# Fused windowed attention and gated unit on one core: output tiles spread over the steps, separate banks and earlier transposes for the first pairs, one mask moved off VectorE

## The chip, the core and the metric

The kernel runs on one core of a Trainium2 chip. Its time is the device time of one execution in microseconds; the time before is 200.69 us, the median of three runs (199.18 to 202.72). The profile is of one more execution, which took 199.83 us and whose profiled span is 198.1 us. All positions "at x us" below are counted from the start of that span.

The engines are named as in the profile: PE is the matrix engine (PEld its weight loads), DVE the vector engine, ACT the scalar engine, POOL the general engine, SP the engine whose queue issues nearly all transfers (SPq).

## What is computed

Attention with a window over 8 batches, 8 heads, 576 positions and a head size of 64, then a gated unit with a causal convolution over the result. Heads 0 to 3 have a plain window of 32 keys; heads 4 to 7 have 32 keys at a distance of 4 (dilated). Cut to what matters:

```python
B, H, S, D = 8, 8, 576, 64
rel = pos[:, None] - pos[None, :]
mask_plain = (rel >= 0) & (rel < 32)
mask_dil = (rel >= 0) & (rel < 128) & (rel % 4 == 0)
attn = softmax(where(mask, q @ k.T / 8, -1e9)) @ v     # per head
x = attn.transpose(0, 2, 1, 3).reshape(B, S, 512)
gate = sigmoid(sum(conv_w[k] * x shifted by 4 - k for k in range(5)))
out = (gate * (x @ w_val)) @ w_out                      # float32
```

## The kernel before

**Pairs and steps.** The work is cut into 32 pairs of heads, four to a batch: c = 0 and 1 are plain, c = 2 and 3 dilated. The main loop has one step for each pair i. Two pairs of one batch and kind make a group g, so there are 16 groups; q, k and v are loaded by group. In a step from 8 on, PE computes the scores of pair i in two halves (L476), ACT takes the exponential (L518), DVE multiplies by the mask (L529), PE multiplies by v (`attn_v`, L531), and DVE normalises (L579, L580). Between these, each step has one convolution (`conv`, 24 matmuls, ACT takes the gate at L654), the transposes of an earlier pair's result (`trans_x`, copied by DVE at L614), transposes of the next group's k or q (`trans_main`, copied by ACT at L407, L404, L418), two value products (`val`, DVE multiplies by the gate at L676), and in some steps one output tile (`out_tile`, L682).

**Output tiles.** An output tile is 128 rows of the result: four matmuls with 512 columns (L687), one eviction on ACT (L692) into one of four buffers `osb`, and one or two stores from the SP queue (L698). There are 36, 18 for each half G of the rows. The values make them available over time, into the list `outs`. In the loop, the condition `c % 2 == 0 and i >= 10` runs one tile in each even step from 10 to 30. All others follow the last step: one after the convolution there, one after each of the last eight values, and the rest in a row.

**The order of the work.** There is no automatic scheduler: each engine executes its instructions in the order in which the program emits them, and each waits in that order. Steps 0 to 7 follow a small table, `program` (L745): X is the transposes of the pair before and its convolution's entry, T the transposes of the next pair's k and q, C a convolution, M and N the two masks, V a value, A the attention output with its normalisation, J a warming matmul, K, Q and R the transposes of group 4, U a cast of v on ACT, and D the convolution's diagonal weights.

**PSUM.** Scores use tiles of two banks, two in rotation (`ps_sc`); all else takes single banks, four in rotation (`ps_one`, through `bank()`). For pairs below `EARLY_AV` = 5 the attention output goes to two single banks, each normalised for itself (L586, L587); from pair 5 on it goes into the second scores tile of the pair, which is then free for the next scores only after L580.

**Transfers.** The SP queue issues loads and stores in program order. A group's loads (k, q, their remainders, v) are issued in even steps, three groups ahead. POOL casts v (`prep_v`, L199 to L208) and, for plain groups from 6 on, k and q (L186).

**The mask of the dilated heads.** `make_bias_d` (L314) is called in step 0. POOL builds bands of 0 and -32768. Its last 32 columns `mb` must also be closed where the parity of key and query differs: `same` holds 0 or -32768 (L263), and DVE takes the minimum (L326). For pairs below `EARLY_M` = 5 the bias is added in PE; later pairs are multiplied by a mask that POOL derives from it (L331).

Of the kernel before, what the change touches and what calls it, by code (L numbers as in the profile page):

```python
# [11 lines left out]
ALU = mybir.AluOpType  # L12
# [11 lines left out]
def kernel(  # L24
# [11 lines left out]
    nc = tc.nc  # L36
# [3 lines left out]
    K = moe_conv_w.shape[0]  # L40
    window = 32
    DIL = 4
    T = S // DIL
    TM = 128
    TR = T - TM
# [6 lines left out]
    CP = T + 2  # L52
    TB = 80
    NP = B * NCH
    EARLY_AV = 5
    EARLY_M = 5
    NEG = -32768.0

# [22 lines left out]
    same = consts.tile([128, 2], BF16, name="same")  # L81
    par_i = consts.tile([128, 2], I32, name="par_i")
# [31 lines left out]
    def bank():  # L114
        return ps_one.tile([128, 512], FP32, name="ps_bank")
# [58 lines left out]
    def load_group(g):  # L174
        for name in ("k", "q"):
            load_main(g, name, 0, 4, nc.sync)
        for name in ("k", "q"):
            load_rest(g, name, nc.sync)
        load_v(g)
# [39 lines left out]
    def pair_info(i):  # L219
        b, c = i // NCH, i % NCH  # L220
        dil = int(c >= NCH // 2)
        return b, c, dil, 2 * b + dil, (c % 2) * 2

    def load_pair(g, a):
        load_main(g, "k", a, a + 2, nc.sync)
        load_main(g, "q", a, a + 2, nc.sync)
        if a == 0:
            load_rest(g, "k", nc.sync)
            load_rest(g, "q", nc.sync)
        load_v(g, a, a + 2)  # L230
# [20 lines left out]
        out=ident, in_=ident, compare_op=ALU.not_equal, fill=1.0,  # L251
        base=0, pattern=[[-1, 128]], channel_multiplier=1,
# [4 lines left out]
        out=ident5, in_=ident5, compare_op=ALU.not_equal, fill=1.0,  # L257
        base=0, pattern=[[-1, 8]], channel_multiplier=1,
    )
    nc.gpsimd.iota(par_i, pattern=[[1, 2]], base=1, channel_multiplier=1)  # L260
    nc.vector.tensor_scalar(out=par_i, in0=par_i, scalar1=1, scalar2=None, op0=ALU.bitwise_and)

    nc.vector.tensor_scalar(  # L263
        out=same, in0=par_i, scalar1=-NEG, scalar2=NEG, op0=ALU.mult, op1=ALU.add)
    for ke in kEs:
        nc.vector.memset(ke[:, :, 0, 96:128], 0.0)
    for et in ets:
# [5 lines left out]
    def band(dst, pattern, base, cm=1):  # L273

        nc.gpsimd.memset(dst, 0.0)
        nc.gpsimd.affine_select(
            out=dst, in_=dst, compare_op=ALU.is_ge, fill=NEG,
            base=base, pattern=pattern, channel_multiplier=-cm,
        )
        nc.gpsimd.affine_select(  # L280
            out=dst, in_=dst, compare_op=ALU.is_ge, fill=NEG,
            base=window - 1 - base, pattern=[[-s, n] for (s, n) in pattern],
            channel_multiplier=cm,
        )
# [4 lines left out]
    for (z, dst) in ((0, bias_1), (1, btmp)):  # L289
# [5 lines left out]
        out=mh, in_=mh, compare_op=ALU.is_ge, fill=0.0,  # L295
        base=96, pattern=[[-1, 2], [1, 4], [4, 24]], channel_multiplier=-2)
# [8 lines left out]
    def make_perm():  # L305

        nc.gpsimd.memset(perm, 0.0)
        pv = perm.rearrange("p (w t) -> p w t", w=2)
        for (x, n, base) in ((0, 16, 0), (16, 32, -32)):
            nc.gpsimd.affine_select(  # L310
                out=pv[:, :, x:x + n], in_=pv[:, :, x:x + n], compare_op=ALU.not_equal, fill=1.0,
                base=base, pattern=[[-n, 2], [-1, n]], channel_multiplier=1)

    def make_bias_d():  # L314
        band(bias_d[:, 0:TM], [[1, TM]], 0)
        nc.gpsimd.tensor_copy(bias_d[:, TM:2 * TM], bias_d[:, 0:TM])

        mb = bias_d[:, 2 * TM:HB].rearrange("p (w t) -> p w t", w=2)
        nc.gpsimd.memset(mb, 0.0)
        for (lo, up) in ((True, 0), (False, 0)):  # L320
            sg = 1 if lo else -1
            base = 2 * (TM - TB) if lo else 2 * (window - 1) - 2 * (TM - TB)
            nc.gpsimd.affine_select(
                out=mb, in_=mb, compare_op=ALU.is_ge, fill=NEG, base=base,
                pattern=[[sg, 2], [2 * sg, TR]], channel_multiplier=-sg)
        nc.vector.tensor_tensor(  # L326
            out=mb, in0=mb, in1=same[:, :, None].to_broadcast([128, 2, TR]), op=ALU.min)

    def make_masks():
        for (m, x) in ((mask_p, bias_p), (mask_d, bias_d)):  # L330
# [20 lines left out]
    def load_weight(src):  # L351
        nc.sync.dma_start(out=w_st, in_=src.rearrange("(c p) n -> p c n", p=128))
# [168 lines left out]
    def apply_mask(i, hf):  # L521
        if i < EARLY_M:
            return
        b, c, dil, g, a = pair_info(i)
        et = st[(i, "et")]
        e3 = et[:, hf, 0:2 * HB].rearrange("p (h n) -> p h n", h=2)
        m = mask_d if dil else mask_p[:, 3 * hf:3 * hf + 3, :].rearrange("p n q -> p (n q)")
        m = m[:, None, :].to_broadcast([128, 2, HB])
        nc.vector.tensor_tensor(out=e3, in0=e3, in1=m, op=ALU.mult)  # L529

    def attn_v(i, hf):  # L531
# [3 lines left out]
        et = st[(i, "et")]  # L535
        if i >= EARLY_AV:
            ps = [st[(i, 1)][:, f, :] for f in range(2)]
# [30 lines left out]
    def normalize(i):  # L568
# [6 lines left out]
        else:  # L575
            dst = xn[0:R].rearrange("p z n h d -> p z (n h) d")
        if i >= EARLY_AV:
            av = st[(i, 1)][0:R, :, 0:6 * AVS].rearrange("p f (x e) -> p f x e", x=6)
# [103 lines left out]
    def out_tile(G, n):  # L682
        w = w_out_b if G == 0 else w_out_s
        ps = bank()
        y0 = 128 * n % (YB * HB)
        for c in range(NCH):
            nc.tensor.matmul(  # L687
                out=ps, lhsT=y_half[G][:, c, y0:y0 + 128], rhs=w[:, c, :],
                start=(c == 0), stop=(c == NCH - 1),
            )  # L690
        osb = out_pool.tile([128, Dm], FP32, name="osb")
        nc.scalar.mul(out=osb, in_=ps, mul=0.5)  # L692
        p = 0
        while p < 128:
            f = 128 * n + p
            b, r, t = f // HB, 2 * G + (f % HB) // T, f % T
            w = min(128 - p, T - t)
            nc.sync.dma_start(  # L698
                out=out[b].rearrange("(t r) n -> r t n", r=4)[r, t:t + w, :],
                in_=osb[p:p + w, :])  # L700
            p += w


    convs, vals, outs = [], [], []
# [16 lines left out]
            outs.append((G, done_out[G]))  # L721
            done_out[G] += 1

    def run_out():
        out_tile(*outs.pop(0))

    def warm(n):
        for _ in range(n):
# [2 lines left out]
    EARLY = 8  # L731

    def next_pair(i, names=("k", "q", "rest")):
# [13 lines left out]
        "X J U J T A J",  # L747
        "X T A J J",
        "X A C C D D J T",
        "X C M N T V V A",  # L750
        "C V M N V X T V A V",
        "C M N X V V A T",
        "C M N X K A Q R J",
    ]
    diags = [2, 3]

# [44 lines left out]
    for i in range(NP):  # L801
        b, c, dil, g, a = pair_info(i)

        if i == 0:
            load_weight(moe_w_val)
            load_pair(2, 0)
        elif i == 1:
            load_pair(2, 2)
        elif i == 2:
            load_pair(3, 0)  # L810
        elif i == 3:
            load_pair(3, 2)
            load_group(4)
        elif i == 4:
            load_weight(moe_w_out)
        if c % 2 == 0 and 5 <= g + 3 < 2 * B:
            load_group(g + 3)

        if i == 0:
            prep_v(0)  # L820
            make_bias_d()
            prep_v(1)
            make_perm()
        elif i < 3:
            prep_v(i + 1)
            if i == 2:
                make_masks()
        elif i == 3:
            cast_val()
            prep_v(4)  # L830
        elif i == 4:
            prep_v(5)
            prep_v(6)
        elif i == 5:
            prep_v(7)
        elif i > 6:
            if i == 8:
                cast_out()
            elif 8 < i < 13:
                for h in range(2):  # L840
                    swap_out(h, i - 9)
            if i < NP - 1:
                prep_v(i + 1)
            if g + 2 < 2 * B and g % 2 == 0:
                cast(g + 2, "k" if a == 0 else "q")
            if 12 <= i < 16:
                swap_val(i - 12)
        scores(i, 0)
        if i == 0:
            trans_rest(0)  # L850
            setup_conv_w()
        scores(i, 1)
        if i == 0:
            make_conv_diag(0)
            make_conv_diag(1)
        if i < EARLY:
            early_rest(i)
            continue
        run_conv(i - 1)
        apply_mask(i, 0)  # L860
        after_x(i - 1)
        if g + 1 < 2 * B:
            trans_main(g + 1, "k" if a == 0 else "q")
        apply_mask(i, 1)
        if c > 0 and vals:
            run_val()
        attn_v(i, 0)
        attn_v(i, 1)
        normalize(i)
        if a == 0 and g + 1 < 2 * B:  # L870
            trans_rest(g + 1)
            if dil:
                even_keys_sb(g + 1)
        if c == 0 and vals:
            run_val()
        if c % 2 == 0 and i >= 10:
            run_out()
        if vals:
            run_val()
    run_conv(NP - 1)  # L880
    if outs:
        run_out()
# [36 lines left out]
```

The softmax here doesn't subtract the row's maximum and nothing guards it: scores larger than these inputs give would overflow.

## Time and profile before

The page of the profile gives busy time in the 198.1 us span:

| engine | busy us | share | instructions |
|---|---|---|---|
| PE | 165.3 | 83% | 2939 |
| PEld | 109.9 | 55% | 2939 |
| DVE | 124.6 | 63% | 313 |
| ACT | 120.6 | 61% | 217 |
| POOL | 99.0 | 50% | 168 |

The core's HBM reads are 31.99 MB and its writes 9.44 MB. The chain of work that ended last is shared by PE (56%), DVE (16%), DMA (10%) and ACT (5%).

How to read what follows: a line of a timeline has the start, the busy time, the engine, the line of the program, the operation, what it writes and reads with shapes, how many instructions were merged, and in brackets how long the engine had stood idle just before and what ended that. A slice of the page is a fortieth of the span, 4.95 us; its digit is the busy share in tenths. Matmuls overlap, so their busy times can add to more than the time that passes.

### The profile page before, as it was taken

The numbers are of one execution on the slowest core, as the hardware profiler recorded it, in microseconds if no ns is written. First come the engines' busy times: TensorE is split into PE (matmuls) and PEld (weight loads), VectorE is DVE, ScalarE is ACT, GpSimd is POOL, SyncE is SP. The second block draws the span as 40 slices with busy tenths as digits, with TensorE's granted clock in tenths as the row PEclk, the third lists the DMA queues.
The fourth block names the chain that finished last, engine by engine and source line by source line (L and its number), as shares of the span: only waits on it lengthen the run. The fifth ranks groups of instructions, "written<-read, shape, count | busy, mean of one in ns | idle before, by whom it ended". The sixth has DMA issues, their size and how long they took to land.

```text
span 198.1 us, 7099 instructions
## 1 busy us (share of the span) xinstructions
PE 165.3 (83%) x2939; PEld 109.9 (55%) x2939; DVE 124.6 (63%) x313; ACT 120.6 (61%) x217; POOL 99.0 (50%) x168
## 2 busy tenths in 40 slices
PE   6557889677788999888789798988989899999950
PEld 2323656456566676656566666666766565554420
DVE  5163566587679787878679777988877783220000
ACT  2223857636857677766576866777787544544651
POOL 7687396079799999784808751897000000000000
PEclk9955999999999999999999999999999999999995
DMA  5999999999978997899399868992021022456885
GB/s 166 245 335 357 249 279 296 235 353 333 239 201 264 249 266 226 242 232 313 85 261 195 261 201 232 246 328 66 3 53 56 3 53 76 159 195 210 253 248 194
DMA packets 48299, 41.90 MB, mean 211 GB/s; under 512 B 6789, under 2 KB 42629, under 8 KB 48266
## 3 DMA queue, kind: packets, MB, share of 16 engines
q1 hardware_dynamic: 47712, 41.30, 76.2%
q8 instruction: 23, 0.38, 0.9%
q10 hardware_dynamic: 554, 0.14, 0.3%
q14 instruction: 10, 0.08, 0.2%
HBM read 31.99 MB, written 9.44 MB: 209 GB/s over the span
## 4 chain that ended last, share of the span: by engine, by line
PE 56%; DVE 16%; DMA 10%; ACT 5%; SPq 4%; issue 4%; POOL 2%; ACTq 0%; POOLq 0%
PE ps_bank L645 10%; PE ps_bank L670 10%; PE ps_bank L687 8%; DVE xn L580 6%; DMA out_dram<-osb 5%; PE ps_bank L392 4%; PE ps_sc L497 3%; PE ps_bank L599 3%; PE ps_sc L550 3%; DMA v_st<-in_v_dram 3%; DMA vPst<-in_v_dram 3%; DVE et L529 3%; PE ps_sc L514 3%; DVE xT L614 2%; SPq L698 2%
## 5 line engine op out<-in xcount | busy, mean ns | idle before, releaser
L518 ACT ACTIVATE et<-ps_sc 128x576 bf16<-128x576 f32 x64 | 39.9, 649 | 29.7 <-PE ps_sc L497 18.2
L692 ACT ACTIVATE osb<-ps_bank 128x512 f32<-128x512 f32 x36 | 21.4, 597 | 27.9 <-PE ps_bank L687 20.4
L676 DVE SCALAR_TENSOR_TENSOR y<-gate,ps_bank 128x288 bf16<-128x288 bf16 x64 | 28.5, 448 | 12.9 <-PE ps_bank L670 9.6
L645 PE MATMUL ps_bank<-xT,conv_diag 64*64 64x288 bf16 (+1 forms) x768 | 26.1, 265 | 0.3 <-DVE xn L587 0.3
L580 DVE TENSOR_TENSOR xn<-ps_sc,rec 128x768 bf16<-128x768 f32 (+1 forms) x27 | 25.8, 955 | 0.9
L654 ACT ACTIVATE gate<-ps_bank 128x288 bf16<-128x288 f32 x64 | 22.9, 415 | 4.9 <-PE ps_bank L645 4.1
L614 DVE COPY xT<-ps_bank 128x576 bf16<-128x576 bf16 x32 | 14.5, 454 | 15.3 <-PE ps_bank L612 8.5
L670 PE MATMUL ps_bank<-xT,w_val_b 128*128 128x288 bf16 x128 | 20.8, 286 | 1.8 <-issue 1.4
L687 PEld LDWEIGHTS <-y 128*128 128x128 bf16 x144 | 13.7, 98 | 13.9 <-issue 1.3
L645 PEld LDWEIGHTS <-conv_diag 64*64 64x64 bf16 x768 | 18.4, 106 | 2.9 <-issue 0.7
L199 POOL CAST vP<-vPst 32x512 bf16<-32x512 f32 x16 | 10.1, 632 | 17.1 <-PE ps_bank L670 7.6
L687 PE MATMUL ps_bank<-w_out_b,y 128*128 128x512 bf16 x72 | 18.0, 379 | 0.1
L687 PE MATMUL ps_bank<-w_out_s,y 128*128 128x512 bf16 x72 | 17.8, 379 | 0.1
L529 DVE TENSOR_TENSOR et<-et,mask_p 128x576 bf16<-128x576 bf16 x26 | 14.5, 561 | 2.5 <-ACT et L518 2.5
L529 DVE TENSOR_TENSOR et<-et,mask_d 128x576 bf16<-128x576 bf16 x28 | 13.7, 490 | 2.2 <-ACT et L518 2.1
L670 PEld LDWEIGHTS <-w_val_b 128*128 128x128 bf16 x128 | 11.4, 97 | 6.5 <-issue 2.6
L200 POOL CAST vP<-vPst 48x768 bf16<-48x768 f32 x16 | 13.8, 863 | 1.0
L201 POOL CAST vP<-vPst 32x768 bf16<-32x768 f32 x16 | 13.7, 856 | 1.0
L497 PE MATMUL ps_sc<-qT,kE 64*64 64x96 bf16 x192 | 9.5, 213 | 5.5 <-DVE xn L580 2.6
L186 POOL CAST k_b<-k_nat 128x512 bf16<-128x512 f32 x10 | 6.1, 639 | 14.0 <-DMA k_nat<-in_k_dram 14.0
L670 PE MATMUL ps_bank<-xT,w_val_s 128*128 128x288 bf16 x80 | 13.1, 286 | 0.0
L497 PE MATMUL ps_sc<-qT,kT 64*64 64x96 bf16 x192 | 9.6, 213 | 3.6 <-DVE qT L462 3.6
(115 smaller groups left out, 320.8 us busy)
## 6 DMA issues: line engine op xcount, KB each, us to landing
k_nat<-in_k_dram SPq DMA_DIRECT2D x12, 512.0 KB, 5.5
q_nat<-in_q_dram SPq DMA_DIRECT2D x12, 512.0 KB, 6.4
vPst<-in_v_dram SPq DMA_DIRECT2D x6, 576.0 KB, 8.4
v_st<-in_v_dram SPq DMA_DIRECT2D x6, 512.0 KB, 6.6
k_nat<-in_k_dram SPq DMA_DIRECT2D x8, 256.0 KB, 5.4
q_nat<-in_q_dram SPq DMA_DIRECT2D x8, 256.0 KB, 5.8
out_dram<-osb SPq DMA_DIRECT2D x8, 256.0 KB, 2.6
out_dram<-osb SPq DMA_DIRECT2D x8, 224.0 KB, 2.9
```

The lines of the kernel that those rows point to most:

```text
L200: nc.gpsimd.tensor_copy(x[0:48], w[0:48])
L497: nc.tensor.matmul(out=ps[D * z:D * z + D, sl, 96 * n:96 * n + 96], lhsT=kk[p0:p0 + D], rhs=t["qT"][p0:p0 + D, a // 2, :, 24 * m:24 * m + 24],
L518: nc.scalar.activation(out=e3, in_=ps[:, :, 0:HB], func=AF.Exp, scale=scale)
L529: nc.vector.tensor_tensor(out=e3, in0=e3, in1=m, op=ALU.mult)
L580: nc.vector.tensor_tensor(out=dst, in0=av[:, :, :, 0:D], in1=rec[0:R, :, :, None].to_broadcast([R, 2, 6, D]), op=ALU.mult)
L614: nc.vector.tensor_copy(xTs[b % NXT][:, c, :, 2:], pr)
L645: nc.tensor.matmul(out=pss[G][D * hp:D * hp + D, o * T:(o + n) * T], lhsT=conv_diag[D * h:D * h + D, c, K - 1 - m, :], rhs=xt[D * h:D * h ...
L654: nc.scalar.activation(out=gate, in_=pss[G][:, 0:HB], func=AF.Tanh, scale=0.5)
L670: nc.tensor.matmul(out=ps[:, 0:HB], lhsT=w[:, mc, c * 128:(c + 1) * 128], rhs=xt[:, mc, 2 * G:2 * G + 2, 2:], start=(mc == 0), stop=(mc == ...
L676: nc.vector.scalar_tensor_tensor(out=y_half[G][:, c, b % YB * HB:(b % YB + 1) * HB], in0=gates.pop((b, c, G)), scalar=1.0, in1=ps[:, 0:HB] ...
L687: nc.tensor.matmul(out=ps, lhsT=y_half[G][:, c, y0:y0 + 128], rhs=w[:, c, :], start=(c == 0), stop=(c == NCH - 1),)
L692: nc.scalar.mul(out=osb, in_=ps, mul=0.5)
```

## The change

It has four parts. The loop runs an output tile in every step after step 8 when one is available, from half 0 only up to step 13, since the weights of half 1 are completed by POOL in steps 9 to 12; in steps with c = 0 the tile stands ahead of the attention output. This is for fewer tiles after the last step. `EARLY_AV` goes from 5 to 8, so that pairs 5 to 7 also use single banks. The table for steps 4 to 7 has transposes earlier. And the dilated mask is built from ones and zeros on POOL alone, multiplied by the parity and then mapped to 0 and -32768, so that DVE has no part in it.

```diff
-    EARLY_AV = 5
+    EARLY_AV = 8
...
-    nc.vector.tensor_scalar(
-        out=same, in0=par_i, scalar1=-NEG, scalar2=NEG, op0=ALU.mult, op1=ALU.add)
+    nc.vector.tensor_copy(same, par_i)
...
-        nc.gpsimd.memset(mb, 0.0)
+        nc.gpsimd.memset(mb, 1.0)
...
-                out=mb, in_=mb, compare_op=ALU.is_ge, fill=NEG, base=base,
+                out=mb, in_=mb, compare_op=ALU.is_ge, fill=0.0, base=base,
...
-        nc.vector.tensor_tensor(
-            out=mb, in0=mb, in1=same[:, :, None].to_broadcast([128, 2, TR]), op=ALU.min)
+        nc.gpsimd.tensor_tensor(
+            out=mb, in0=mb, in1=same[:, :, None].to_broadcast([128, 2, TR]), op=ALU.mult)
+        nc.gpsimd.tensor_scalar(
+            out=mb, in0=mb, scalar1=-NEG, scalar2=NEG, op0=ALU.mult, op1=ALU.add)
...
-    def run_out():
-        out_tile(*outs.pop(0))
+    def run_out(i=NP):
+
+        for j, (G, n) in enumerate(outs):
+            if G == 0 or i > 13:
+                out_tile(*outs.pop(j))
+                return True
+        return False
...
-        "X C M N T V V A",
-        "C V M N V X T V A V",
-        "C M N X V V A T",
-        "C M N X K A Q R J",
+        "X C T M N V V A",
+        "T C M N X V V A V V",
+        "C T X M N V V A",
+        "C K Q X M N A R J",
...
+        ahead = c == 0 and i > EARLY and run_out(i)
         if c > 0 and vals:
             run_val()
         attn_v(i, 0)
...
-        if c % 2 == 0 and i >= 10:
-            run_out()
+        if i > EARLY and not ahead:
+            run_out(i)
```

## The prediction

> **What bounds the kernel now.** I read the page's forty slices first, then busy time in five stretches, then the timelines of single engines where those change character. PE has high digits everywhere; the DMA engines are full up to about 130 us, and idle again until the end.
>
> ```profile
> PE   6557889677788999888789798988989899999950
> ...
> PEclk9955999999999999999999999999999999999995
> DMA  5999999999978997899399868992021022456885
> ```
>
> The stretches are start-up, steps 1 to 8, steps 9 to 31, and the two halves of the tail. Columns: window, length, then busy us (and count) of PE, PEld, DVE, ACT, POOL, then clock, DMA share, GB/s.
>
> ```profile
> 0.00:18.00 18.00, 10.59 (x104) 5.33 (x104) 8.07 (x36) 5.27 (x8) 13.74 (x40) 0.75 0.96 270
> ...
> 59.60:162.80 103.20, 93.16 (x1946) 66.95 (x1941) 83.59 (x198) 72.78 (x129) 57.44 (x87) 1.00 0.70 184
> 162.80:176.70 13.90, 13.72 (x123) 7.97 (x123) 5.25 (x11) 6.20 (x12) 0.00 (x0) 1.00 0.42 134
> 176.70:198.10 21.40, 14.30 (x65) 6.16 (x63) 0.00 (x0) 10.11 (x17) 0.00 (x0) 0.89 0.72 222
> ```
>
> Three things stand out. In the last 21.4 us nothing runs but output tiles: DVE and POOL have no work, and PE is busy for only 14.3 of it. The timeline of ACT there shows evictions that wait for a store to free a buffer:
>
> ```profile
> 175.60 0.60 ACT L692 ACTIVATE osb<-ps_bank 128x512 f32<-128x512 f32 x1 [0.76 <-PE ps_bank L687]
> ...
> 190.95 1.33 ACT L692 ACTIVATE osb<-ps_bank 128x512 f32<-128x512 f32 x2 [1.06 <-DMA out_dram<-osb]
> ...
> 193.97 0.60 ACT L692 ACTIVATE osb<-ps_bank 128x512 f32<-128x512 f32 x1 [0.52 <-DMA out_dram<-osb]
> ```
>
> At the start DVE stands still for 4.33 us for the mask of the dilated heads, with the copies that PE needs behind it in the queue:
>
> ```profile
> 6.88 0.41 DVE L402 COPY qT<-ps_bank 128x512 bf16<-128x512 bf16 x1
> 11.63 0.19 DVE L326 TENSOR_TENSOR bias_d<-bias_d,same 128x32 bf16<-128x32 bf16 x1 [4.33 <-POOL bias_d L323]
> 11.73 0.28 DVE L459 COPY kT<-ps_bank 128x128 bf16<-128x128 bf16 x1
> ```
>
> In between, PE stops about once in each odd step, ahead of the second half of the next scores, because their bank still holds the attention output that the normalising multiply L580 reads. After an even step, which has an output tile, it doesn't stop there. The timeline of PE, end of steps 25, 26 and 27:
>
> ```profile
> 138.11 0.28 PE L514 MATMUL ps_sc<-qA,kA 64*128 64x128 bf16 x4 [0.49 <-DVE xn L580]
> ...
> 140.78 1.03 PE L687 MATMUL ps_bank<-w_out_b,y 128*128 128x512 bf16 x4
> ...
> 142.38 0.27 PE L514 MATMUL ps_sc<-qA,kA 64*128 64x128 bf16 x4
> ...
> 146.46 0.23 PE L497 MATMUL ps_sc<-qT,kE 64*64 64x96 bf16 x2 [0.57 <-DVE xn L580]
> ```
>
> **What the Trainium skill says.** "Perfetto Trace Analysis", Optimization Strategy: where the contended engine changes over time, interleaving the regimes can help. The trace agrees that there are two: PE, DVE and ACT at 93, 84 and 73 of 103 us in steps 9 to 31, then stores alone. "TensorE: Matmul & The Clock Gate", Part 1: the array drops to half rate after an idle window of some 3.4 us and returns after as long a busy one. The trace shows a clock of 0.50 from 9.5 to 19 us, around a PE pause from 8.8 to 12.2. "DMA: Bandwidth & Descriptors", Issuing engines are not separate DMA queues: all transfers share the same 16 engines, so earlier stores meet the loads; the share in the busiest microseconds is already above 1.0 here.
>
> **Part 1, 11 output tiles leave the tail.** Following the loop by hand, before has 11 tiles in even steps 10 to 30 and 25 after the last step. After has 22 (steps 9 to 31 without 13) and 14 after. The first nine of either tail lie between the values and one convolution, 13.9 us (162.8 to 176.7), where ACT waits for PE alone; that stays. Then come 16 tiles in 21.4 us before, and 5 after. The ACT pace of those 16 is (193.97 - 177.23)/15 = 1.12 us a tile, set by stores. So 21.4 - 11 x 1.12 = 9.1 us. From the other side, 5 tiles at PE's 0.86 us are 4.3, plus an eviction 0.60, an issue 0.47 and a landing of 2.65 to 3.83 (chain of waits): 8.0 to 9.2. I take 9.1: **-12.3 us**, bounds -12.2 and -13.4.
>
> **Part 2, the same 11 tiles enter steps 9 to 31.** All 11 new ones fall in odd steps. Each adds 0.86 us of PE (132.28 to 133.14 in the timeline) just after the attention output, where PE stops for about 0.53 (0.49 and 0.57 above). Net 0.33 each, 3.7 in all. In steps 12, 16, 20, 24 and 28 the tile moves ahead of the attention output, where step 24 shows a 0.21 us stop for the mask: -1.0. Behind it there, one transpose group (0.12), two values (0.98) and half the scores (0.23) make 1.33 us, which still cover the 1.22 us of reciprocal and multiply (131.77 to 132.99). ACT gets 11 x 0.60 = 6.6 us more in a stretch where it is busy 73 of 103; the eviction runs while PE does a value, ahead of the next exponential, as it does now after even steps. Stores: 11 x 256 KB = 2.9 MB more, about 12 us at the tail's 222 GB/s over 103 us whose share is 0.70. They queue behind loads, so PE and DVE may now and then find data late; I add 1.0 for that. Sum **+3.7 us**. Bounds: +1.5, if all stops in the odd steps vanish and nothing else slows, and 11 x 0.86 = +9.5 if none does.
>
> The queue of loads needs its own sentence. SP issues in order, and a store waits on it for its eviction (69.8 us over 25 waits in the list of SP's waits). The next group's five or six loads stand behind the store of the step before, which is now an odd step, so they leave up to a step (4.3 us) later. A group is loaded three groups, six steps, ahead of use; k and q land in 5.5 and 6.4 us and the casts on POOL want them two steps later at the earliest, about 8.7 us. I cost it at nothing: the slack of 2 us or more hides it, thinly.
>
> **Part 3, the mask leaves DVE.** L459 could start when its transposes end, 7.61 + 0.28 = 7.89 us, and starts at 11.73: 3.8 us. Behind it, in a chain without slack, are L462, the scores, the next keys, the value cast on ACT and the first attention output (16.13). That output also needs POOL's casts, done at 9.62, so they don't bind. The loads are ahead: the keys of pair 1 are issued by 3.5 us, and 256 KB land in 5.4 to 5.8. POOL gets two operations on 128x32: no multiply is in the trace; between an affine select there (0.25) and a 128x288 scalar operation (0.43) each, I take 0.5 for both, beside a cast of pair 1 that ends at 14.2, some 4 us before its reader even if that moves up. PE's pause shortens, so the clock may not fall: the chain has 5.4 us of PE work at half rate between 12.2 and 19.6, at most 2.7 us. I take 0.2 of it. **-4.0 us**, bounds -2.0 (loads or other copies hold the next steps) and -6.5.
>
> **Part 4, steps 4 to 7.** Separate banks for pairs 5 to 7 free the score tile: the 0.50 us stop at 44.66 goes and others like it may, at two short normalising chains of 0.19 + 0.55 in place of 0.23 + 0.95 us (+0.25 of DVE each). Transposes earlier: ACT's copies then run before PE needs them (1.16 us at 49.26, 0.67 at 53.59). Against it, only four single banks rotate, and three transposed tiles ahead of a convolution make its second bank wait for ACT's copies behind two exponentials (1.2 + 0.9 us). Stops seen in steps 5 to 7 add to some 3.9 us; I take a quarter: **-1.0**, bounds -3.0 and +1.5.
>
> **Sum.** 200.7 - 12.3 + 3.7 - 4.0 - 1.0 = **187.1 us**.
>
> **The rivals.** First (0.66): the sum. Second (0.20): PE is the bound everywhere, so the moved tiles cost their full 9.5 us in the steps and part 4 gives nothing: 200.7 - 12.3 + 9.5 - 4.0 = 193.9. For it: PE is busy 93 of 103 us; against: the clean run of step 26 into 27. Third (0.08): besides, the start-up gain is lost to loads, as the DMA is full from 2 to 54 us: 197.9, no visible change. Against: no wait for a load in the chain between 12 and 89 us. Fourth (0.06), slower: later loads and fuller DMA stop POOL and then PE once per remaining group, eight times about 1.5 us (as in the 5.3 us steps 15 and 16, where the chain names a load), on top of the third: 209.9.
>
> **How the numbers follow.** The range 183 to 196 spans the best ends of parts 2 and 3 to beyond the second rival; it leaves out the last two (0.14). Faster by over 2% (below 196.7) is the first two, 0.86; no change 0.08; slower 0.06.
>
> **What would show it.** DVE's 4.33 us wait is gone and the first attention output stands near 12 us. Steps 9 to 31 take 105 to 108 us in place of 103, with no stop on L580 in odd steps. From the last convolution to the end there are about 23 us in place of 35. Against me would be waits of POOL or PE for k_nat or v tiles between 60 and 140 us, or steps of 5 us each.

## The result and the profile after

The changed kernel takes 184.59 us, median of four runs (183.21 to 186.14), beside 200.49 us (199.18 to 202.72) for four runs of the kernel before on the same chip: a ratio of 0.920, with a 95% interval of 0.910 to 0.931. It is faster, and the forecast of 187.1 with its range of 183 to 196 holds. Here and below a median is over all runs, while ratios and intervals leave out runs over 1.5% slower than the fastest of their kernel, so the two need not agree exactly. The profiled execution has a span of 181.5 us where before had 198.1, 16.6 us less.

First the page's forty slices of the kernel after (a slice is 4.54 us now), then the busy time of the main stretch and of the tail, with the same columns as before.

```profile
PE   6768988998399999989999999999999999999990
...
PEclk9978999999969999999999999999999999999997
DMA  5999999899999999999597999999961112146685
```

```profile
54.99:158.32 103.33, 100.84 (x1965) 70.77 (x1980) 84.87 (x198) 76.12 (x140) 64.66 (x98) 1.00 0.82 223
158.32:181.50 23.18, 18.14 (x141) 9.86 (x142) 4.54 (x10) 9.93 (x19) 0.00 (x0) 0.94 0.59 171
```

In the slices PE's digits are nearly all 9 in the second half, and one digit of 3 stands at slice 11 (45 to 50 us): that is step 7, and it matters below. In the windows PE is now busy 100.84 of the 103.33 us of steps 9 to 31, where it was busy 93.16 of 103.20, and the stretch has not become longer. The span is cut here at three marks that both kernels have (us): the first attention output, the start of step 9's convolution, and the start of the first convolution after step 31. The prediction calls this one the last; one more follows it, 6.4 us later in both kernels.

| stretch | before | after | difference | forecast |
|---|---|---|---|---|
| start to first attention output | 16.13 | 11.75 | -4.4 | part 3: -4.0 |
| from there to step 9's convolution | 43.47 | 43.24 | -0.2 | part 4: -1.0 |
| steps 9 to 31 | 103.16 | 103.33 | +0.2 | part 2: +3.7 |
| first convolution after step 31 to end | 35.34 | 23.18 | -12.2 | part 1: -12.3 |

They sum to -16.6. The timeline of DVE at the start, after, has no wait for the mask:

```profile
6.57 0.41 DVE L402 COPY qT<-ps_bank 128x512 bf16<-128x512 bf16 x1
7.62 0.29 DVE L459 COPY kT<-ps_bank 128x128 bf16<-128x128 bf16 x1 [0.63 <-PE ps_bank L451]
```

The copy L459, which started at 11.73 before, starts at 7.62. The mask's two new operations on POOL take 0.24 (L324) and 0.22 us (L326), at 12.59 and 12.92, when nothing waits for them.

In the timeline of PE after, steps 9 to 31, four stops of more than 0.15 us are left, 1.26 us in all. The one on L580, at 78.07, comes at the end of step 13, the only step from 9 on that runs no tile:

```profile
78.07 0.29 PE L514 MATMUL ps_sc<-qA,kA 64*128 64x128 bf16 x4 [0.51 <-DVE xn L580]
85.93 0.30 PE L564 MATMUL ps_sc<-vA,et 128*128 128x65 bf16 x4 [0.27 <-DVE et L529]
...
152.50 0.30 PE L564 MATMUL ps_sc<-vA,et 128*128 128x65 bf16 x4 [0.24 <-DVE et L529]
...
156.67 0.30 PE L564 MATMUL ps_sc<-vA,et 128*128 128x65 bf16 x4 [0.24 <-DVE et L529]
```

In the same stretch before there were 22 such stops, 9.8 us in all: 11 on the normalising multiply L580 (5.6), eight on a mask L529 (2.5), one put down to "issue" (0.90), one to a load of v (0.61) and one to L676 (0.17). So the stretch had 8.6 us of stops that are gone, and PE has 7.7 us more work by the windows: the eleven tiles lie in the holes. (The profile of the change has 25 fewer matmul records than weight loads, so 7.7 is too little; the same 22 tiles in kernels with all records, below, give 8.2 to 8.9.) In the tail ACT waits for a store once, for 0.46 us, where the kernel before has nine such waits, 6.5 us in all.

### The profile page after: what moved, and what is told of

Read it like the earlier page. It is cut to its first block, busy times and chain, and to the rows that moved or that the text cites. A ratio compares the mean times of both kernels' runs of the same rounds, so it can differ in the third digit from the quotient of the medians.

```text
span 181.5 us, 7070 instructions
## 1 busy us (share of the span) xinstructions
PE 163.6 (90%) x2914; PEld 110.0 (61%) x2939; DVE 123.7 (68%) x318; ACT 117.1 (65%) x217; POOL 100.1 (55%) x170
## 4 chain that ended last, share of the span: by engine, by line
PE 73%; DVE 11%; DMA 5%; ACT 5%; issue 2%; SPq 2%; ACTq 0%
PE ps_bank L687 14%; PE ps_bank L670 13%; PE ps_bank L645 12%; PE ps_bank L392 5%; DMA q_nat<-in_q_dram 4%; PE ps_sc L497 3%; PE ps_bank L599 3%; PE ps_bank L665 3%; PE ps_sc L550 3%; PE ps_sc L514 3%; PE ps_sc L564 3%; DVE et L529 2%; PE ps_bank L612 2%; DVE xn L587 2%; DVE xT L614 2%
## 5 line engine op out<-in xcount | busy, mean ns | idle before, releaser
L518 ACT ACTIVATE et<-ps_sc 128x576 bf16<-128x576 f32 x64 | 38.7, 648 | 24.0 <-PE ps_sc L497 16.1
L676 DVE SCALAR_TENSOR_TENSOR y<-gate,ps_bank 128x288 bf16<-128x288 bf16 x64 | 28.0, 449 | 11.4 <-PE ps_bank L670 9.2
L645 PE MATMUL ps_bank<-xT,conv_diag 64*64 64x288 bf16 (+1 forms) x768 | 28.6, 270 | 0.7 <-DVE xn L587 0.6
L580 DVE TENSOR_TENSOR xn<-ps_sc,rec 96x768 bf16<-96x768 f32 (+1 forms) x24 | 22.9, 955 | 0.8
L614 DVE COPY xT<-ps_bank 128x576 bf16<-128x576 bf16 x32 | 14.6, 455 | 11.9 <-PE ps_bank L612 5.7
L645 PEld LDWEIGHTS <-conv_diag 64*64 64x64 bf16 x768 | 19.6, 108 | 4.5 <-DVE qB L471 1.3
L670 PE MATMUL ps_bank<-xT,w_val_b 128*128 128x288 bf16 x128 | 19.8, 286 | 0.2 <-DVE xT L614 0.2
L687 PEld LDWEIGHTS <-y 128*128 128x128 bf16 x144 | 12.9, 97 | 11.4 <-issue 0.5
L529 DVE TENSOR_TENSOR et<-et,mask_d 128x576 bf16<-128x576 bf16 x28 | 15.0, 541 | 2.5 <-ACT et L518 2.5
L529 DVE TENSOR_TENSOR et<-et,mask_p 128x576 bf16<-128x576 bf16 x26 | 13.7, 531 | 2.5 <-ACT et L518 2.5
L670 PEld LDWEIGHTS <-w_val_b 128*128 128x128 bf16 x128 | 11.7, 98 | 3.9 <-issue 0.2
L201 POOL CAST vP<-vPst 32x768 bf16<-32x768 f32 x16 | 13.4, 838 | 1.0
L670 PE MATMUL ps_bank<-xT,w_val_s 128*128 128x288 bf16 x80 | 13.1, 286 | 0.1
L186 POOL CAST k_b<-k_nat 128x512 bf16<-128x512 f32 x10 | 6.3, 650 | 12.3 <-DMA k_nat<-in_k_dram 6.2
L203 POOL CAST vP<-vPst 32x768 bf16<-32x768 f32 x14 | 12.5, 893 | 0.6
L205 POOL CAST vA<-v_st 128x512 bf16<-128x512 f32 x16 | 11.4, 715 | 2.0 <-DMA v_st<-in_v_dram 1.8
```

What stands on the lines that cost most here:

```text
L201: nc.gpsimd.tensor_copy(x[64:96], w[32:64])
L518: nc.scalar.activation(out=e3, in_=ps[:, :, 0:HB], func=AF.Exp, scale=scale)
L580: nc.vector.tensor_tensor(out=dst, in0=av[:, :, :, 0:D], in1=rec[0:R, :, :, None].to_broadcast([R, 2, 6, D]), op=ALU.mult)
L614: nc.vector.tensor_copy(xTs[b % NXT][:, c, :, 2:], pr)
L645: nc.tensor.matmul(out=pss[G][D * hp:D * hp + D, o * T:(o + n) * T], lhsT=conv_diag[D * h:D * h + D, c, K - 1 - m, :], rhs=xt[D * h:D * h ...
L670: nc.tensor.matmul(out=ps[:, 0:HB], lhsT=w[:, mc, c * 128:(c + 1) * 128], rhs=xt[:, mc, 2 * G:2 * G + 2, 2:], start=(mc == 0), stop=(mc == ...
```

## The experiments

Each kernel below computes the whole result. Ratios are to runs of the kernel before on the same chip. "The stretch of steps 5 to 7" is from the end of the attention output of step 4 to the end of that of step 8; it holds nearly everything that the new table and the single banks touch (row 4 of the table begins before it).

### The tiles alone

The theory: PE's stops in the steps sum to more than I counted, so the eleven tiles are free there. Its rival: the tiles cost what I forecast, about 4 us, and some other part of the change pays for it. The kernel before, with only the loop changed (the body of `run_out`, left out here, is that of the change):

```diff
-    def run_out():
-        out_tile(*outs.pop(0))
+    def run_out(i=NP):
...
+        ahead = c == 0 and i > EARLY and run_out(i)
...
-        if c % 2 == 0 and i >= 10:
-            run_out()
+        if i > EARLY and not ahead:
+            run_out(i)
```

> The kernel before with the new placing of output tiles alone (22 in steps 9 to 31 and 14 after them; mask, banks and table as before). Theory A: the 11 tiles that enter the steps fill stops of PE, of which before has about 10 us there, so they cost nothing, and the tail gives 12.2 us: about 188.3 us. Rival B: they cost the forecast 0.3 to 0.4 us each, and the profile of before merely held some 3 us of pauses by chance: about 192.

Measured: 188.99 us against 201.96, a ratio of 0.941 (0.933 to 0.948), so about -11.9 us by the ratio. Its windows, steps 9 to 31 and the tail:

```profile
60.23:163.30 103.07, 101.35 (x1986) 70.49 (x1978) 84.65 (x198) 75.94 (x140) 61.50 (x92) 1.00 0.77 216
163.30:186.30 23.00, 18.25 (x143) 9.85 (x142) 4.54 (x10) 9.94 (x19) 0.00 (x0) 0.96 0.59 173
```

The steps take 103.07 us with 22 tiles in them, and the tail 23.00. The eleven added tiles cost nothing that shows, without the other parts of the change: the first theory holds. PE is busy 8.2 us longer than before, 0.75 a tile, and the stops of the stretch fell to 1.7 us. Nor did the kernel before hold its 9.8 us of stops by chance: the next two kernels have its loop, and their traces show 8.4 and 10.5 us in this stretch.

### The mask alone

```diff
-    nc.vector.tensor_scalar(
-        out=same, in0=par_i, scalar1=-NEG, scalar2=NEG, op0=ALU.mult, op1=ALU.add)
+    nc.vector.tensor_copy(same, par_i)
...
-        nc.gpsimd.memset(mb, 0.0)
+        nc.gpsimd.memset(mb, 1.0)
...
-                out=mb, in_=mb, compare_op=ALU.is_ge, fill=NEG, base=base,
+                out=mb, in_=mb, compare_op=ALU.is_ge, fill=0.0, base=base,
...
-        nc.vector.tensor_tensor(
-            out=mb, in0=mb, in1=same[:, :, None].to_broadcast([128, 2, TR]), op=ALU.min)
+        nc.gpsimd.tensor_tensor(
+            out=mb, in0=mb, in1=same[:, :, None].to_broadcast([128, 2, TR]), op=ALU.mult)
+        nc.gpsimd.tensor_scalar(
+            out=mb, in0=mb, scalar1=-NEG, scalar2=NEG, op0=ALU.mult, op1=ALU.add)
```

> The kernel before with the mask built on POOL alone. Theory A: all work behind DVE's 4.3 us wait moves up by 4.1 to 4.4 us and nothing takes it back: about 196.1 us. Rival B: the loads, which keep the DMA engines full up to 54 us, take it back in steps 3 to 8: 198.5 or more.

Measured: 195.67 us, ratio 0.974 (0.968 to 0.980), about -5.2 (-6.4 to -3.9): the first theory. The first attention output starts at 12.22, and steps 9 to 31 take 102.99. The stretch of steps 5 to 7 takes 19.89 where before has 21.38, although nothing in it was changed. Of that, 1.42 us is one pause of PE in the kernel before, at 39.62, which has no releaser in the profile ("issue") and is absent here; I have no cause for it. In the kernel with the tiles alone, where the stretch took 20.77, PE pauses for 1.11 us at the same line (L670).

### Banks and table alone

```diff
-    EARLY_AV = 5
+    EARLY_AV = 8
...
-        "X C M N T V V A",
-        "C V M N V X T V A V",
-        "C M N X V V A T",
-        "C M N X K A Q R J",
+        "X C T M N V V A",
+        "T C M N X V V A V V",
+        "C T X M N V V A",
+        "C K Q X M N A R J",
```

> The kernel before with single banks for pairs 5 to 7 and the new table for steps 4 to 7 together. Theory A: the two give about what the traces show between the first attention output and step 9, 0.2 us, so about 200.3. Rival B: they give the forecast 1 us or more by themselves (199.5 or less), and less beside the mask, because loads then bind steps 4 to 8.

Measured: 202.09 us (22 runs), ratio 1.010 (1.007 to 1.013): no gain, and by the ratio a loss of about 2 us, which neither theory had (the medians, 202.09 and 201.96, differ by less). The stretch takes 21.05 where before has 21.38, or 19.96 without its pause. A new stop of PE stands in it, ahead of the attention output of step 7:

```profile
52.25 0.30 PE L564 MATMUL ps_bank<-vA,et 128*128 128x65 bf16 x4 [1.99 <-DVE et L529]
```

### What the table does, with the rest of the change in place

The changed kernel with old banks, or the old table, or both. The rivals: banks and table each do little, or the banks gain and the table takes it away.

```diff
-    EARLY_AV = 8
+    EARLY_AV = 5
...
-        "X C T M N V V A",
-        "T C M N X V V A V V",
-        "C T X M N V V A",
-        "C K Q X M N A R J",
+        "X C M N T V V A",
+        "C V M N V X T V A V",
+        "C M N X V V A T",
+        "C M N X K A Q R J",
```

> The changed kernel with single banks only for pairs 0 to 4 and the old table for steps 4 to 7. If the two early edits are worth 0.2 us: about 184.8. If they matter only beside the earlier start (rival B of the run before turned round): 186 or more.

> The changed kernel once more, as the base of the three beside it. Nothing new: about 184.6 us.

> The changed kernel with single banks for pairs 0 to 4 only, the new table kept. If the separate banks are a gain (stops of 0.5 us on L580 in three steps, less 0.25 us of DVE each): 0.5 to 1 us slower than the changed kernel. If the banks cost, by crowding the four single banks: 0.5 us or more faster.

> The changed kernel with the old table for steps 4 to 7, the separate banks kept. Theory A (the loss sits in the new table: in step 7 the key copies of group 4 stand ahead of the masks on DVE, and the attention output waits 2.1 us for the masks): 1 to 2 us faster than the changed kernel, 183 us. Theory B (the loss sits in the banks): as the changed kernel or slower.

| kernel after with | us | ratio (95%) | stretch of steps 5 to 7 | mean PE clock there |
|---|---|---|---|---|
| old banks, old table (the whole diff above) | 183.73 | 0.902 (0.893 to 0.911) | 19.5 | 1.00 |
| nothing undone | 183.82 | 0.918 (0.913 to 0.923) | 21.5 | 0.92 |
| old banks, new table | 186.17 | 0.927 (0.922 to 0.931) | 22.3 | 0.85 |
| new banks, old table | 182.06 | 0.908 (0.904 to 0.912) | 18.8 | 1.00 |

The first row ran together with the parts alone, the other three together; the ratio of the first rests on two of its six runs. The new table lengthens the stretch by some 2.7 us with either bank setting, and in the times it costs 1.8 us: the intervals of rows two and four don't touch. So the table's loss is shown. A gain from the banks is not. With either table they shorten the stretch by 0.75 us (19.51 to 18.77, 22.25 to 21.5), but in the four executions that have the change's own steps 4 to 8 (two of the change, and the last two kernels below) it took 20.4 to 22.3 us. By the ratios the banks gain 0.9% with the new table, where the intervals just meet, and nothing with the old one. Row one is below both times that were expected of it, and row three is 2.3 us slower than row two, more than the 0.5 to 1 expected.

Where the 2.7 us go can be read from the windows of the stretch, first with nothing undone, then with the new banks and the old table:

```profile
34.29:55.79 21.50, 17.22 (x366) 13.00 (x367) 16.05 (x44) 12.45 (x25) 11.81 (x18) 0.92 1.10 302
34.23:53.00 18.77, 15.21 (x367) 11.75 (x367) 16.01 (x44) 12.82 (x25) 8.89 (x12) 1.00 1.08 291
```

PE stands idle for 4.28 us in the first and 3.56 in the second, only 0.7 us more. The other 2.0 us are busy time: the same matmuls take 17.22 us in place of 15.21, at a mean clock of 0.92 in place of 1.00. In the first kernel PE ran at half rate for some 3.4 us near the end of the stretch, which is what a mean of 0.57 over 4.00 us comes to:

```profile
51.50:55.50 4.00, 3.57 (x60) 3.00 (x62) 2.32 (x6) 2.13 (x5) 3.32 (x5) 0.57 1.16 280
```

### Which row of the table

Row 7, "C K Q X M N A R J", emits the transposes of group 4 ahead of the scores' masks M and N, and the copies of those keys (L433) with them. Two kernels: the change with the old row 7 only, and the change with the old table and the new row 7 only.

```diff
-        "C K Q X M N A R J",
+        "C M N X K A Q R J",
```

> The changed kernel with the table's row for step 7 alone as before, so that the masks of pair 7 come ahead of the key copies of group 4. Theory A: the 2.1 us wait goes and stops of about 0.7 to 1.4 us at the next scores come back: 0.7 to 1.4 us faster, 183.5 us. Theory B: no change.

```diff
-        "X C T M N V V A",
-        "T C M N X V V A V V",
-        "C T X M N V V A",
+        "X C M N T V V A",
+        "C V M N V X T V A V",
+        "C M N X V V A T",
```

> The changed kernel with separate banks and the old table, but the new row for step 7 (key copies of group 4 ahead of the masks). If that row makes the loss: the wait for the mask ahead of the attention output of pair 7 is back at about 2 us, the stretch from the end of attention output 4 to that of 8 is about 2 us longer than the 18.8 us with the old table, and the time is 1 to 2 us above 182.1. If other rows make it: 182 us and some 19 us.

Measured: with the new row 7 alone in the old table 184.33 us, ratio 0.918 (0.912 to 0.925), the same as the whole change; the stretch takes 22.05 at a mean clock of 0.85. The timelines of DVE and of PE in that kernel:

```profile
46.78 1.09 DVE L433 COPY kE<-ps_bank 128x288 bf16<-128x288 bf16 x4 [3.45 <-ACT kT L407]
48.15 1.66 DVE L529 TENSOR_TENSOR et<-et,mask_d 128x576 bf16<-128x576 bf16 x2
```

```profile
49.08 0.40 PE L564 MATMUL ps_bank<-vA,et 128*128 128x65 bf16 x4 [2.76 <-DVE et L529]
```

DVE stands for 3.45 us ahead of the key copies because ACT's copy of kT isn't done (ACT does two exponentials and two gates first); the masks of pair 7 are behind them in DVE's order, and PE's attention output waits 2.76 us for the masks. With the old table the same two operations stand the other way round, and PE has no such wait (0.30 us at most); here DVE's timeline in the change with the old table:

```profile
45.30 1.69 DVE L529 TENSOR_TENSOR et<-et,mask_d 128x576 bf16<-128x576 bf16 x2 [1.19 <-ACT et L518]
47.53 1.08 DVE L433 COPY kE<-ps_bank 128x288 bf16<-128x288 bf16 x4 [0.18 <-ACT kT L407]
```

Over all fourteen traces the picture is the same. In the seven with the new row 7 PE waits 2.0 to 2.8 us for the masks of step 7, and a half-rate interval of some 3.4 or 6.8 us begins between 0.5 us before and 2.4 us after the end of that wait; the seven with the old row have neither in this stretch, where their longest stop is 1.4 us. The mean clocks of whole runs agree: the versions of the changed kernel that have the new row average 0.963 to 0.974 over their runs, those with the old row 0.979 to 0.992. That the row brings both the wait and the slow clock is shown; that the wait is what lowers the clock is the likely reading, and no run tests it apart.

The other kernel, with only row 7 put back, didn't settle as clearly: its profile has no mask wait and a stretch of 19.17 us, 2.3 less than the change, but its median is 183.78 (ratio 0.915, 0.910 to 0.920), the same as the change's 183.82. Its profiled execution was the fastest of its six (181.60) and that of the change the slowest of its six (185.13). Its clock was 0.991 in the profiled execution and 0.968 to 0.987 in the other five, so in these PE spent longer at half rate; where, no trace shows, and why they don't gain stays open. That row 7 makes a loss in the old table is shown by the trace and agrees with the times (182.06 against 184.33, the intervals just meet); that rows 4 to 6 do nothing isn't shown.

From this follows a version that should beat both: the old table's order of masks, with the transposes behind the masks but ahead of the attention output in rows 6 and 7 too (T in row 6, Q in row 7).

```diff
-        "X C T M N V V A",
-        "T C M N X V V A V V",
-        "C T X M N V V A",
-        "C K Q X M N A R J",
+        "X C M N T V V A",
+        "C V M N V X T V A V",
+        "C M N X T V V A",
+        "C M N X K A Q R J",
```

> The changed kernel with separate banks and a table that keeps the old order of masks and convolutions, but has the transposes behind the masks and ahead of the attention output in steps 6 and 7. If the 1.12 us stop for ACT's copy of q at the start of step 7's second scores and the 1.10 us stop of the remainder's transposes go without a wait for masks: 181 us, the stretch from attention output 4 to 8 some 17.5 us. If the copies on ACT or DVE hold up something else: 182 us or more.

Measured: 181.42 us, ratio 0.901 (0.894 to 0.907), stretch 18.44. It is the fastest kernel of the study by its median and faster than the change (0.918, 0.913 to 0.923); from the change with the old table (0.908, 0.904 to 0.912), or with the old banks too (0.902), it can't be told apart. Of the two stops that were to go, the one on ACT's copy of qA is gone; one of 1.0 us on ACT's copy of qT remains, and one as long on L462.

### Where a tile stands in a step

If the tiles are free because each fills the time in which DVE normalises, one that stands ahead of the attention output in every step should not be. If PE only has spare time somewhere in a step, the place makes no difference.

```diff
-        ahead = c == 0 and i > EARLY and run_out(i)
+        ahead = i > EARLY and run_out(i)
```

> The changed kernel with the output tile ahead of the attention output in every step, not only where c = 0; the same tiles, the same stores. If tiles are free because they fill PE's stop on the normalising multiply behind the attention output, that stop of about 0.5 us comes back in some 17 steps: the stretch of steps 9 to 31 grows from 103.3 to 108 to 112 us, time 189 to 193. If they are free because the stretch is bound by something else (loads, POOL), it stays at 103.3 and the time at 184.

Measured: 194.8 us, ratio 0.968 (0.959 to 0.976), a little more than the first theory's 189 to 193. Steps 9 to 31, then PE's timeline there:

```profile
58.17:171.53 113.36, 101.93 (x1970) 70.78 (x1980) 83.82 (x196) 79.12 (x140) 61.52 (x92) 1.00 0.69 195
```

```profile
103.84 0.29 PE L514 MATMUL ps_sc<-qA,kA 64*128 64x128 bf16 x4 [0.51 <-DVE xn L580]
108.74 0.28 PE L514 MATMUL ps_sc<-qA,kA 64*128 64x128 bf16 x4 [0.48 <-DVE xn L580]
...
114.25 0.23 PE L497 MATMUL ps_sc<-qT,kE 64*64 64x96 bf16 x2 [0.58 <-DVE xn L580]
```

The same tiles in the same steps cost 10.0 us more, in the ratios too. PE has 20 stops again, 10.0 us in all: 17 on L580 (8.4) and three on L676 (1.6). The place decides. The stops on masks, on the other hand, are gone, since a tile ahead of the attention output covers those. That is the use of the tile ahead of it in the c = 0 steps.

### No tile in the loop

```diff
-        ahead = c == 0 and i > EARLY and run_out(i)
...
-        if i > EARLY and not ahead:
-            run_out(i)
```

> The changed kernel with all 36 output tiles after the last step. The tail grows by 22 tiles at 1.12 us, 24.6 us. Theory A (tiles fill stops of PE, DVE sets the pace without them): steps 9 to 31 stay within 2 us of 103.3 us, so the time is 207 to 209. Theory B (each tile costs PE time in the steps): the stretch is 7 us shorter or more, the time 202 or less.

Measured: 205.94 us, ratio 1.024 (1.015 to 1.033), between the two theories: the steps are 3.5 us shorter. Steps 9 to 31, and the tail:

```profile
55.82:155.61 99.79, 86.17 (x1899) 63.78 (x1892) 86.49 (x198) 68.18 (x118) 63.85 (x97) 1.00 0.73 174
155.61:202.40 46.79, 37.57 (x227) 18.41 (x230) 5.29 (x11) 22.73 (x40) 0.00 (x0) 0.97 0.67 203
```

Steps 9 to 31 take 99.8, 103.2 and 103.3 us with 0, 11 and 22 tiles (the 11 are those of the kernel before, none of them ahead of the attention output). So 22 tiles cost (103.33 - 99.79)/22 = 0.16 us each in the steps, and in the tail (46.79 - 23.18)/22 = 1.07 each. With all 22 ahead of the attention output it was (113.36 - 99.79)/22 = 0.62 each. Without tiles PE stops for 13.6 us in the steps, 8.4 of it on L580 and 3.4 on masks; with them 1.3 us are left. "Perfetto Trace Analysis", Optimization Strategy, of the Trainium skill says that interleaving regimes with different contended engines can help; here it is worth 0.9 us for each tile moved.

## Why the prediction was right, point by point

**Part 1, the tail: right.** Forecast -12.3 from 11 tiles at 1.12 us; measured -12.2 in the profiles, and 1.07 a tile when all 22 are put back. The tail is 23.2 us where "about 23 us" stood.

**Part 2, the tiles in the steps: right in mechanism, wrong in size.** Forecast +3.7, measured +0.2, which lies even below my bound of +1.5, for which I had given no working. Three terms of the sum failed; together they make about the 3.5 us.
- "where PE stops for about 0.53": the sample (steps 25 to 27) was right for the stops on L580, which sum to 5.6 us over eleven steps, as 11 x 0.53 does. But I counted no other stops beyond five of 0.21 on masks, so some 6.8 us. All stops of the stretch came to 9.8 us, and 8.6 of them went, 1.8 more than I had counted. Those on masks were as long as 0.61 earlier in the kernel, in the phase in which loads and casts run, and the sample lay behind it.
- "Each adds 0.86 us of PE": by the windows of the kernels whose traces have all matmul records it is 0.75 to 0.81, 0.6 to 1.2 us less over eleven.
- "I add 1.0 for that", for late data: no stop of PE on a load is left after. ACT waits once in the steps for a store (1.44 us at 87.24), and no stop of PE stands behind it. Steps 9 to 31 took 102.9 to 103.6 us in every kernel that has the tiles where the change puts them.

That the tile behind the attention output covers the normalising, which this step rested on, is shown by the kernel with every tile ahead of it (+10.0 us), and by step 13, which has no tile and keeps its stop. The sign "105 to 108 us" failed with the size, and "no stop on L580 in odd steps" held in all but step 13.

**The queue of loads, costed at nothing: right.** Counted from the start of step 9, the next six groups of loads leave 1.3 to 6.5 us later, and POOL's waits put down to k_nat fell from 14.0 to 6.2 us (another 5.9 us before the same casts are now put down to PE). "DMA: Bandwidth & Descriptors", Issuing engines are not separate DMA queues, of the Trainium skill led me to expect the stores to meet the loads; they do share, 0.82 of the engines' time in place of 0.70, at no cost that shows.

**Part 3, the mask: right, and a little small.** Forecast -4.0; the first attention output comes 4.4 us earlier, near 12 us as written. Over all traces it stands at 16.1 to 17.3 in the three kernels with the old mask and at 11.6 to 13.2 in the eleven with the new one. Alone the mask gave -5.2 by its ratio, inside the bounds and with the 4.4 inside its interval. My 0.2 us for the clock can't be judged, since the half-rate interval moves between executions of the same start: 9 to 19 us in before, some 11.3 to 15 in after, none in two others. "TensorE: Matmul & The Clock Gate", Part 1, of the Trainium skill gives some 3.4 us as the idle time that leads to it. The traces differ, and the measurement decides: in the kernel before the clock fell at 9.1, 0.3 us into the pause, and in step 7 with the new row the longest wait was 2.0 to 2.8 us. So the idle time alone doesn't let one foresee which execution has it.

**Part 4, banks and table: wrong.** Forecast -1.0; the stretch of steps 5 to 7 didn't get shorter (21.4 before, 21.1 and 21.5 in two profiles after), though the mask alone brought it to 19.9. The stops that I had named did go. Here the two in the kernel before, then the same matmuls after, and the stop that came in their place:

```profile
44.66 0.28 PE L514 MATMUL ps_sc<-qA,kA 64*128 64x128 bf16 x4 [0.50 <-DVE xn L580]
...
49.26 0.29 PE L514 MATMUL ps_sc<-qA,kA 64*128 64x128 bf16 x4 [1.16 <-ACT qA L418]
```

```profile
38.15 0.27 PE L514 MATMUL ps_sc<-qA,kA 64*128 64x128 bf16 x4
...
42.05 0.28 PE L514 MATMUL ps_sc<-qA,kA 64*128 64x128 bf16 x4
...
47.01 0.30 PE L564 MATMUL ps_bank<-vA,et 128*128 128x65 bf16 x4 [2.09 <-DVE et L529]
```

So "Transposes earlier: ACT's copies then run before PE needs them" held. The step that failed is what I set against it. I had ACT's copies behind two exponentials delay PE's bank; they delay DVE, which has the masks queued behind the key copies, and PE waits 2.0 to 2.8 us for the masks. I had looked at what is queued behind the waiting instruction for PE and ACT, and not for DVE. And I had counted the clock in the start alone: beside the mask alone PE's idle time in the stretch even fell, from 4.6 to 4.0 us, but the half-rate interval made its matmuls take 17.1 us in place of 15.3. The table as a whole cost 1.8 us in the times. The single banks end the 0.50 us stop on L580 by themselves (with the old table it is there with the old banks and gone with the new), but that this wins time is not shown.

**The sum.** Part 2 came out 3.5 us better than forecast, part 3 0.4 better, part 4 0.8 worse, part 1 0.1 worse. The row of part 4 is flattered by the pause of 1.42 us that the kernel before had there; without it the row would be a loss of 1.2 us. That part 4's miss took back some of part 2's is luck. The second rival, full cost of the tiles in the steps, fell with the first window above; the third fell with the earlier start, and the fourth with steps 9 to 31, which have no stop of PE on a load.

**What stays open.** What the "issue" pauses of PE of 0.9 to 1.4 us are, whether the single banks gain anything, whether the wait in step 7 is what lowers the clock, and why the kernel with only row 7 put back isn't faster in its median. None was tried further.

## What to carry to other kernels

Independent work on the bounding engine is nearly free where it stands right behind the instruction whose consumer that engine waits for next (0.16 us for a tile of 0.86), and costs most of its time where it stands ahead of it (0.62): find the stop, ask which engine fills it and where its work starts, and put the filler there. Add up the stops of the whole stretch by what ends them rather than multiplying a clean sample, since the quiet end of a kernel shows shorter ones. When an order is changed to get an operation done earlier, follow it on every engine that has a part in it: a copy moved ahead waits in order with all that is behind it, here the masks. And compare busy time as well as stops: several short stops became one of 2 us, and more was lost to the slow clock than to added idle time.

## What was not expected of the hardware

The time of one and the same kernel on one chip spread from 198.5 to 207.2 us over 27 runs of the kernel before, and with six runs of a changed kernel the intervals reach 0.8 to 1.8 us to either side, so that differences under 1 us couldn't be told apart. The position of PE's half-rate interval in the start moves by some microseconds between executions. So does the first attention output, from 11.6 to 13.2 us in kernels that are alike up to there, but not together with it: the two latest, at 13.19, are in the two executions whose start has no such interval. A half-rate interval stood beside waits of 2.0 to 2.8 us in step 7, in seven of seven traces. And the mask multiplies of one shape aren't of one length: two of 128x576 take 0.82 us at 42.68 and 1.67 us at 48.40 in the second profile of the changed kernel. POOL has nothing to do from 42.6 to 43.6 us and is busy 1.84 of the 1.90 us from 48.3; that its casts are the cause was not tried.
